# A fused HGRN2 attention and low-rank mixer: the hand-over from batch 0 to batch 1, with other steps between TensorE's products and with VectorE and ScalarE left to the scheduler

## The chip, the cores and the metric

One core of one Trainium2 chip runs the whole program. The metric is the device time of one execution in microseconds (us); lower is better. Five engines of the core matter here: TensorE (PE in the profile, its weight loads PEld), VectorE (DVE), ScalarE (ACT), GpSimd (POOL) and SyncE (SP), which issues nearly all the DMAs. Every engine executes its own instructions in order; the engines wait for each other with semaphores.

## The reference

Two blocks, one after the other, in float32. The attention block runs a gated recurrence over 768 steps for 4 batches of 8 heads of 48 columns; the mixer block mixes over time with a product of rank 32 and then over channels with two dense layers.

```python
batch, n_heads, seq, head_dim = (4, 8, 768, 48)
f = 1.0 / (1.0 + np.exp(-f_logit))
for t in range(S):
    state = f[:, :, t, :, None] * state + np.einsum('bhd,bhe->bhde', k[:, :, t], v[:, :, t])
    y[:, :, t] = np.einsum('bhd,bhde->bhe', q[:, :, t], state)
x = y.transpose(0, 2, 1, 3).reshape(B, S, H * D)          # (4, 768, 384)
u = x + (x.transpose(0, 2, 1) @ U @ V).transpose(0, 2, 1)  # U: 768 x 32, V: 32 x 768
ch = np.maximum(u @ w_ch1, 0.0) @ w_ch2                    # 384 -> 1536 -> 384
return u + ch
```

## The kernel before

**Units and batches.** Attention works in 16 units, each a pair of heads of one batch: unit n belongs to batch n // 4. A unit has a front and a rear. The front turns the inputs into operands: "gates" (the forget logits are transposed on VectorE, L766, and go through the sigmoid on ScalarE, L875 and L876), "keep" (a scan over time, L880, and four small operations, L885, L887, L888, L890), "keys" (a transpose L766 and a product L809), "read_back" (a second scan, L898) and "queries" (again L766 and L809). The rear computes scores, states and outputs on TensorE, with the scan of the states on VectorE (L1055) and copies on ScalarE (L1010, L1016, L1038, L1095).

**The mixer.** For each batch, `low_rank` forms x'U on TensorE (L184, tile ph) and ScalarE copies it out (L192, tile h); `added_up` adds its four parts with one product (L197) and ScalarE copies again (L199). `mix_blocks` multiplies by V (tile pu) and VectorE adds the result to x (L204): for batch 0 two blocks at a time, for the later batches four blocks at once in `mix_four` (L221) and then the last two (L214). `turn` transposes x on TensorE (L288, tile put), ScalarE copies the result to uT (L289). Then come the first dense layer, L300 (tile pz) with ReLU on ScalarE (L335), and the second one.

**Second products.** The 768 rows of a batch are six blocks of 128, taken as three pairs. A pair's second layer is either done plainly (L355, tile po) or, with sums of operands formed before, in seven instead of eight smaller products (L389, tile pw). Batch 0 does its first two pairs plainly and its third pair in seven. `seven` has four steps: step 0, 1 and 2 hold two products each (12 matmul instructions of the program, six per product), step 3 holds one. VectorE reads each step's pw with additions (L204, tiles w_y and o), and ScalarE copies one part of step 0 (L405). Step 1 needs a difference of second-layer weights that VectorE makes in place (L571), step 2 another (L572). Finished rows are stored by SP (L343).

**Around the change.** `start_mixer(1, after, early, late)` interleaves two things on TensorE: the end of batch 0 (`after`, the four steps of `seven` for its third pair) and the start of batch 1's mixer (`m.before`: `low_rank`, `added_up`, `mix_blocks`, three times `turn`). `early` and `late` are front pieces of the next units: read_back and queries of unit 9, gates and keep of unit 10. In the kernel before, `after` is `m.halved(...)`, seven pieces of one product each, so that `added_up` stands between the two products of step 1 and the mixing stands ahead of step 2.

**What sets the order.** TensorE's order is the order in which the program is written (`manual_schedule` for TensorE, over the whole kernel). VectorE's and ScalarE's order is the written order as well within an inner `manual_schedule` block, which in the kernel before reaches to the end of the first four pieces of batch 1's attention. After that block a scheduler orders VectorE and ScalarE by its own estimate of when operands are ready; additions marked `high_priority` (those through `add`) are favoured by it.

**Buffers.** The tiles pw, pu and put, and sc, y, ds and pt of attention, share three double-bank PSUM buffers (pool `ps_big`); ph, pz, po and two of the four tiles of `mix_four` share two single-bank ones (`ps_mm`). A buffer is written again when its last reader has finished. The tile `whole` (L1016) has one buffer, which the scan L1055 reads.

Of the kernel before, what the change touches and what calls it, by code (L numbers as in the profile page):

```python
# [576 lines left out]
def factored_path(ctx, tc, q, k, v, f_logit, moe_U, moe_V, moe_w_ch1, moe_w_ch2, out, ok):  # L577
# [10 lines left out]
    NBL = S // P  # L588
    HP = H // 2
# [29 lines left out]
    late = const.tile([P, 7, S], F32, name="late")  # L619
# [22 lines left out]
    def load(n, *names):  # L642

        b, hp = divmod(n, HP)
        for nm in names:
            if nm == "v":
                v_tiles[n] = three.tile([P, NBL, 2, D], F32, name="v_nat")
            for par in range(2):
                head = src[nm][b, 2 * hp + par]
                if nm in "kq" and n < HP:  # L650
                    if par == 0:
                        nc.sync.dma_start(
                            out=packed(n, nm).rearrange("p (h t) -> p h t", h=2),
                            in_=src[nm][b, 2 * hp : 2 * hp + 2].rearrange("h (p c) d -> p h (c d)", p=P),
                        )
                    continue
                if nm == "v" and par:

                    for s in range(2):
                        nc.sync.dma_start(  # L660
                            out=v_tiles[n][(1 - s) * C : (2 - s) * C, :, par, :],
                            in_=head.rearrange("(c s p) d -> s p c d", s=2, p=C)[s],
                        )
                    continue
                if nm == "v" or n < TURNED:
                    dst = v_tiles[n] if nm == "v" else nat[n % 2][nm]
                    nc.sync.dma_start(out=dst[:, :, par, 0:D], in_=head.rearrange("(c p) d -> p c d", p=P))
                    continue
                head = head.rearrange("(c i) d -> i c d", i=NB)
                for part in range(2):  # L670
                    p0 = par * PAD + part * NB
                    n_ch = min(NB, D - part * NB)
                    nc.sync.dma_start(
                        out=raw[n % 2][nm][p0 : p0 + NB, :].rearrange("p (c d) -> p c d", d=NB)[:, :, 0:n_ch],
                        in_=head[:, :, part * NB : part * NB + n_ch],
                    )
# [63 lines left out]
    early = len(weights)  # L740
# [169 lines left out]
    def mixer(b):  # L910
        return Mixer(tc, b, x_tiles[b], U, V, w1, w2, sums, ident, blocks, out, two, three, zp, ps_big, ps_mm,
                     b == 0, z_all, room if b >= B - 2 else None, FEWER - (b - B + 2) * NCH // 4)
# [11 lines left out]
    def sum_of_w(i):  # L924
        if i == 0:
            flat = late.rearrange("p a s -> p (a s)")
            w_places.extend(flat[:, j * FG : (j + 1) * FG] for j in range(7 * S // FG))
            w_places.extend(t[:, 0:FG] for t in fz + [added])
            flat = z_all[:, NFC:, :].rearrange("p i t -> p (i t)")
            w_places.extend(flat[:, j * FG : (j + 1) * FG] for j in range(3))  # L930
            assert max(W_PLACES) < len(w_places)
        n, p, sign, q = W_SUMS[i]
        nc.vector.tensor_tensor(w_node(n), w_node(p), w_node(q), ALU.add if sign == "+" else ALU.subtract)
# [171 lines left out]
    def front(n, *names):  # L1105

        if n >= NU:
            return []
        if n not in ahead:
            names_of = ("gates", "keep", "keys", "read_back", "queries", "gates_end", "unpack_k", "unpack_q")  # L1110
            ahead[n] = dict(zip(names_of, prepare(n)))
        return [ahead[n].pop(nm) for nm in names if nm in ahead[n]]

    def rear(n, *names):

        if not 0 <= n < NU:
            return []
        if n not in here:
            here[n] = dict(zip(("kept", "states", "scan", "scores", "read", "inner", "mask", "spread"), attend(n)))
        return [here[n].pop(nm) for nm in names if nm in here[n]]  # L1120

    def joined(*groups):

        groups = [g for g in groups if g]
        for _ in groups[1:]:
            yield lambda: None
        if groups:
            yield lambda: [f() for g in groups for f in g]

    def steps(first, last):  # L1130

        def behind(n):

            return HP + 3 <= n < NU - 1

        for n in range(first, last):
            if n < NU:
                yield from joined(rear(n - 2, "inner"), rear(n - 1, "scores"), rear(n, "kept"))
            else:
                for piece in rear(n - 2, "inner") + rear(n - 1, "scores"):  # L1140
                    yield lambda: None
                    yield piece
            if behind(n):
                yield from front(n, "read_back", "queries")
            if n + 1 < NU and n + 1 not in v_tiles:
                load(n + 1, "v")
            yield from front(n + 1, "gates", "keep", "keys")
            yield from joined(rear(n - 1, "read"), rear(n, "states", "scan"))
            if not behind(n + 1):
                yield from front(n + 1, "read_back", "queries")  # L1150
            if n + 1 == last:
                yield from rear(n - 1, "inner")
                if n + 2 < NU:
                    load(n + 2, "v")

    def attention(pieces, fill):

        for piece in pieces:
            fill()
            piece()  # L1160
        fill.rest()

    def beside(pieces, calls):

        for i, piece in enumerate(pieces):
            yield piece
            while calls and calls[0][0] <= i:
                calls.pop(0)[1]()
        assert not calls

    def start_mixer(b, after, early=(), late=()):

        m = mixer(b)
        n = len(after) // 4
        early, late = ([(0, f) for f in of] for of in (early, late))
        if late:
            pieces = after[:2] + m.before[:1] + early + after[2:3] + m.before[1:2] + after[3:4] + m.before[2:3] + late
            pieces += after[4:] + m.before[3:]
        else:
            pieces = after[:n] + m.before[:1] + after[n : 2 * n] + m.before[1:2] + after[2 * n : 3 * n]  # L1180
            pieces += m.before[2:3] + after[3 * n :] + m.before[3:]
        for _, piece in pieces:
            piece()
        return m
# [4 lines left out]
    with tc.manual_schedule(engines={nc.vector.engine, nc.scalar.engine}):  # L1189
# [21 lines left out]
        def room_for(first, last):  # L1211
            for i in range(first, last, 2):
                t = zp.tile([P, NFC // 2, 2 * P], F32, name="zw").rearrange("p i t -> p (i t)")
                nc.scalar.copy(t[:, 0:1], x_tiles[0][:, 0, 0:1])
                spare.extend([t.bitcast(U64)[:, 0:WP], t.bitcast(U64)[:, WP : 2 * WP]])
            for load_w in weights[early + first : early + last]:
                load_w[0]()
# [5 lines left out]
        for n in range(HP):  # L1223
            last = n + 1 == HP
            pieces = rear(n - 1, "scan") + front(n, "unpack_q", "keys") + rear(n, "spread") + rear(n - 1, "read")
            if last:
                pieces = [w[0] for w in weights[1:early]] + [lambda: room_for(0, 2)] + pieces + join[:1] + halves[1:2]
# [27 lines left out]
        m = mixer(0)  # L1255
# [44 lines left out]
            f()  # L1300
        first, third, others = to_sum
        todo = m.second(0) + [(0, first), (0, third)] + m.second(1)[:6] + m.ready(2) + m.second(1)[6:] + [(0, others)]
        after = m.halved(NBL // 2 - 1)

        attention(second, Fill(todo, 10 + 10 * HP - (len(start) + len(m.firsts) - 1 - EARLY)))
        n = 2 * HP + 2
        m = start_mixer(1, after, front(n - 1, "read_back", "queries"), front(n, "gates", "keep"))
        pieces, fill = steps(n - 1, 3 * HP + 1), Fill(m.main, 10 * HP - 3)
        for _ in range(4):
            fill()  # L1310
            next(pieces)()
    for b in range(2, B - 1):
        if b > 2:
            pieces, fill = steps(b * HP + 1, (b + 1) * HP + 1), Fill(m.main, 10 * HP)
        after = m.after
        attention(pieces, fill)
        m = start_mixer(b, after)
# [3 lines left out]
    for i in range(early_sums):  # L1321
        sum_of_w(i)
    pieces = beside(steps((B - 1) * HP + 1, NU + 1),
                    [(t, lambda i=i: sum_of_w(i)) for i, t in enumerate(turns, early_sums)])
# [375 lines left out]
```

## Time and profile before

| | |
|---|---|
| median of 3 runs | 473.17 us (472.33 to 473.63) |
| the profiled execution | 473.17 us, of which 471.4 us are the span from its first to its last instruction |
| busy, PE / DVE / ACT / POOL | 96% / 76% / 35% / 11% of the span |
| granted TensorE clock | 1.0 |
| DMA | 34.37 MB, 73 GB/s over the span |

The span can be cut at the place of the change. Batch 0's last products and the start of batch 1's mixer lie between 150 and 172 us. The costliest groups of the page show what the kernel's time consists of; each line gives the program line, the engine, the operation, the tiles, the number of instructions, the busy time and the mean of one in ns, and after the bar the idle time before them and what ended it:

```profile
L300 PE MATMUL pz<-uT,w 128*128 128x256 f32 x492 | 111.6, 382 | 0.3 <-DVE w_y L204 0.2
L389 PE MATMUL pw<-w,z_all 128*128 128x192 f32 x228 | 39.5, 327 | 0.0
L389 PE MATMUL pw<-zw,w_raw 128*128 128x192 f32 x168 | 30.1, 329 | 1.9 <-DVE zw L571 1.9
L880 DVE TENSOR_TENSOR_SCAN late<-fz,late 128x768 f32<-128x768 f32 x12 | 21.1, 1754 | 12.0 <-ACT fz L875 11.9
L898 DVE TENSOR_TENSOR_SCAN late<-fz,other 128x768 f32<-128x768 f32 x12 | 22.0, 1835 | 0.1
```

A matmul of the program on float32 operands shows as two records of the trace. Matmul durations overlap, so the pace of a run of them is read from their starts, not from the mean of one.

### The profile page before, as it was taken

The page shows a single profiled execution, that of the slowest core. Times are in us where ns is not written, and L with a number is a line of the kernel's source. Part 1 is how long each engine was busy: PE and PEld are TensorE (multiplying, and loading weights), DVE is VectorE, ACT ScalarE, POOL GpSimd, SP SyncE. Part 2 cuts the span into 40 slices and gives each one's busy share as a digit, 9 for nine tenths or more (in the row PEclk, how much of TensorE's full clock was granted, in tenths as well). Part 3 has the DMA queues.
Part 4 walks back from the last instruction along what each step waited for, and adds up shares of the span by engine and source line. Part 5 has one row for each costly group of instructions (what it writes and reads, how often), then busy time and mean ns, then how long its engine had stood idle before and what let it go on. Part 6 is the DMA issues. An engine that isn't in the chain of part 4 may idle for free.

```text
span 471.4 us, 13114 instructions
## 1 busy us (share of the span) xinstructions
PE 454.6 (96%) x5675; PEld 400.2 (85%) x5675; DVE 357.9 (76%) x596; ACT 166.3 (35%) x320; POOL 53.9 (11%) x60
## 2 busy tenths in 40 slices
PE   8998999999979789999999999999999999999996
PEld 6886888876657678899898888989989999999996
DVE  5768788979999957766756568977897896858652
ACT  6775776562332034322322323431221311112200
POOL 2002445634110100101010100120000000000000
PEclk9999999999999999999999999999999999999999
DMA  9939998587667533503542130100000000000001
GB/s 198 203 109 214 217 216 177 147 124 102 111 96 110 84 60 42 84 6 75 74 64 60 26 60 3 27 4 19 19 2 1 33 1 19 18 0 35 1 34 39
DMA packets 148584, 34.37 MB, mean 73 GB/s; under 512 B 136934, under 2 KB 146982, under 8 KB 148518
## 3 DMA queue, kind: packets, MB, share of 16 engines
q1 hardware_dynamic: 147718, 33.29, 36.5%
q8 instruction: 47, 0.77, 0.7%
q10 hardware_dynamic: 800, 0.15, 0.2%
q14 instruction: 19, 0.16, 0.1%
HBM read 28.70 MB, written 4.72 MB: 71 GB/s over the span
## 4 chain that ended last, share of the span: by engine, by line
PE 77%; DVE 15%; issue 4%; ACT 2%; DMA 1%; POOL 0%; SPq 0%; DVEq 0%; ACTq 0%; POOLq 0%
PE pw L389 24%; PE pz L300 20%; PE pp L496 12%; PE po L355 5%; PE y L1071 2%; PE sc L979 2%; PE ds L1030 2%; PE y L1089 2%; PE pt L789 2%; PE pt L839 1%; DVE w_raw L204 1%; PE pt L1006 1%; DVE added L1055 1%; DVE late L880 1%; DVE x L204 1%
## 5 line engine op out<-in xcount | busy, mean ns | idle before, releaser
L300 PE MATMUL pz<-uT,w 128*128 128x256 f32 x492 | 111.6, 382 | 0.3 <-DVE w_y L204 0.2
L300 PEld LDWEIGHTS pz<-uT,w 128*128 128x128 f32 x492 | 91.7, 190 | 13.1 <-PE pw L389 0.5
L1059 POOL COPY st<-added 128x576 f32<-128x576 f32 x12 | 17.8, 1484 | 193.4 <-DVE added L1055 193.4
L389 PE MATMUL pw<-w,z_all 128*128 128x192 f32 x228 | 39.5, 327 | 0.0
L389 PEld LDWEIGHTS pw<-w,z_all 128*128 128x128 f32 x228 | 37.2, 190 | 0.6
L101 POOL TENSOR_TENSOR w<-w_y,w_r 128x384 int32<-128x384 int32 x24 | 31.5, 1311 | 37.0 <-DVE w_y L100 22.5
L335 ACT ACTIVATE z_all<-pz 128x512 f32<-128x512 f32 x33 | 19.6, 596 | 40.6 <-PE pz L300 40.2
L389 PE MATMUL pw<-zw,w_raw 128*128 128x192 f32 x168 | 30.1, 329 | 1.9 <-DVE zw L571 1.9
L880 DVE TENSOR_TENSOR_SCAN late<-fz,late 128x768 f32<-128x768 f32 x12 | 21.1, 1754 | 12.0 <-ACT fz L875 11.9
L389 PEld LDWEIGHTS pw<-zw,w_raw 128*128 128x128 f32 x168 | 27.3, 190 | 2.7 <-issue 2.2
L489 ACT ACTIVATE other<-other 128x512 f32<-128x512 f32 x18 | 11.3, 631 | 40.3 <-DVE other L204 40.3
L992 DVE TENSOR_TENSOR A<-sc,causal 128x768 f32<-128x768 f32 x16 | 15.2, 951 | 13.5 <-PE sc L979 13.5
L898 DVE TENSOR_TENSOR_SCAN late<-fz,other 128x768 f32<-128x768 f32 x12 | 22.0, 1835 | 0.1
L875 ACT ACTIVATE fz<-late 128x756 f32<-128x756 f32 x10 | 8.3, 832 | 33.8 <-DVE late L766 33.8
L489 ACT ACTIVATE z_all<-z_all 128x512 f32<-128x512 f32 x12 | 7.6, 631 | 34.1 <-DVE z_all L204 34.1
L1038 ACT COPY added<-ds 48x576 f32<-48x576 f32 (+2 forms) x29 | 17.8, 618 | 4.7 <-PE ds L1030 4.2
L496 PE MATMUL pp<-v_nat,late 128*128 128x128 f32 x152 | 19.1, 275 | 0.0
L98 DVE TENSOR_SCALAR w_y<-w_y 128x384 f32<-128x384 f32 (+3 forms) x27 | 12.1, 448 | 8.9 <-ACT w_y L91 8.9
L1071 PEld LDWEIGHTS y<-st,qT 48*64 48x64 f32 x704 | 13.6, 137 | 6.0 <-issue 3.9
L389 PE MATMUL pw<-w,other 128*128 128x192 f32 x108 | 18.5, 326 | 0.0
L1016 ACT COPY whole<-whole 128x576 f32<-128x576 f32 x16 | 10.8, 672 | 21.3 <-DVE added L1055 21.1
L496 PEld LDWEIGHTS pp<-v_nat,late 128*128 128x128 f32 x152 | 18.0, 192 | 0.0
(234 smaller groups left out, 913.0 us busy)
## 6 DMA issues: line engine op xcount, KB each, us to landing
w_raw<-in_moe_w_ch_dram SPq DMA_DIRECT2D x18, 384.0 KB, 3.7
out_dram<-o SPq DMA_DIRECT2D x17, 192.0 KB, 1.9
v_nat<-in_v_dram SPq DMA_DIRECT2D x16, 144.0 KB, 3.0
v_nat<-in_v_dram SPq DMA_DIRECT2D x32, 72.0 KB, 3.5
zw<-in_moe_w_ch_dram SPq DMA_DIRECT2D x6, 384.0 KB, 4.8
out_dram<-o SPq DMA_DIRECT2D x14, 96.0 KB, 2.2
w<-in_k_dram SPq DMA_DIRECT2D x4, 288.0 KB, 3.7
w<-in_q_dram SPq DMA_DIRECT2D x4, 288.0 KB, 4.7
```

The source lines that it names most:

```text
L101: nc.gpsimd.tensor_tensor(dst.bitcast(I32), shaped(y.bitcast(I32)), shaped(r), ALU.add)
L300: nc.tensor.matmul(pm[:, i * 2 * P : (i + 1) * 2 * P], lhsT=w1[:, m, o : o + P], rhs=uT[a][:, m, :], start=(m == 0), stop=(m == NDC - 1))
L335: nc.scalar.activation(z[a, c][:, k : k + 2, :].rearrange("p i t -> p (i t)"), pm, AF.Relu)
L355: nc.tensor.matmul(pm, lhsT=z[a, i // NI][:, i % NI, s * P : (s + 1) * P], rhs=w2[:, i, :], start=(i == 0), stop=(i == NFC - 1))
L389: nc.tensor.matmul(W["pm"][:, n * HM : (n + 1) * HM], lhsT=lhs[:, i, :], rhs=rhs[i] if isinstance(rhs, list) else rhs[:, i, :], start=(i = ...
L489: nc.scalar.activation(dst, dst, AF.Relu, scale=float(SIGNS[n]))
L496: nc.tensor.matmul(pm[:, i, r * P : (r + 1) * P], lhsT=room["w"](wn)[:, r * P : (r + 1) * P], rhs=x_node(a, xn), start=((xn, wn) == of[0]) ...
L880: nc.vector.tensor_tensor_scan(backwards(X, S - 1, S), backwards(f, S, S), backwards(ends, S - 1, S), 0.0, ALU.mult, ALU.add,)
L898: nc.vector.tensor_tensor_scan(Y, f[:, 0:S], starts, 0.0, ALU.mult, ALU.add)
L1038: nc.scalar.copy(added[r, 1:].rearrange("p (e c s) -> p e c s", c=NBL, s=2)[:, e], ds[r, :, 0 : NBL * D].rearrange("p s (c e) -> p e c s", ...
L1059: nc.gpsimd.tensor_copy(st, states.rearrange(by_e, c=NCH))
L1071: nc.tensor.matmul(o(c % 2, par, c // 2), lhsT=T["q"][rows[par], chunk[c]], rhs=T["st"][rows[par], c, :], start=(c <= 2), stop=False, skip ...
```

## The change

`halved` is no longer used here: `after` is `m.after`, the four whole steps of `seven`. `start_mixer` has one order for all batches; `early` follows `low_rank`, `late` follows step 2 and stands ahead of the mixing. The call of `start_mixer(1, ...)` and the first four pieces of batch 1's attention leave the inner block, so that the scheduler orders VectorE and ScalarE there. The mixing of batch 1 is done four blocks at once before and after.

```diff
         m = mixer(b)
         n = len(after) // 4
         early, late = ([(0, f) for f in of] for of in (early, late))
-        if late:
-            pieces = after[:2] + m.before[:1] + early + after[2:3] + m.before[1:2] + after[3:4] + m.before[2:3] + late
-            pieces += after[4:] + m.before[3:]
-        else:
-            pieces = after[:n] + m.before[:1] + after[n : 2 * n] + m.before[1:2] + after[2 * n : 3 * n]
-            pieces += m.before[2:3] + after[3 * n :] + m.before[3:]
+        pieces = after[:n] + m.before[:1] + early + after[n : 2 * n] + m.before[1:2] + after[2 * n : 3 * n] + late
+        pieces += m.before[2:3] + after[3 * n :] + m.before[3:]
         for _, piece in pieces:
             piece()
         return m
...
-        after = m.halved(NBL // 2 - 1)
+        after = m.after
 
         attention(second, Fill(todo, 10 + 10 * HP - (len(start) + len(m.firsts) - 1 - EARLY)))
-        n = 2 * HP + 2
-        m = start_mixer(1, after, front(n - 1, "read_back", "queries"), front(n, "gates", "keep"))
-        pieces, fill = steps(n - 1, 3 * HP + 1), Fill(m.main, 10 * HP - 3)
-        for _ in range(4):
-            fill()
-            next(pieces)()
+    n = 2 * HP + 2
+    m = start_mixer(1, after, front(n - 1, "read_back", "queries"), front(n, "gates", "keep"))
+    pieces, fill = steps(n - 1, 3 * HP + 1), Fill(m.main, 10 * HP - 3)
+    for _ in range(4):
+        fill()
+        next(pieces)()
```

Built, the two programs hold the same compute instructions, and their order differs in this stretch alone:

| engine | order before | order after |
|---|---|---|
| TensorE | step 0, L184, half of step 1, L197, other half, mixing L221 and L214, step 2, step 3, L288 | step 0, L184, step 1, L197, step 2, mixing L221 and L214, step 3, L288 |
| VectorE | keys of unit 9 (L766, L809), po's o, L1055, L571, L572, step 0, L898, L766 and L809 of unit 9's queries, step 1, four additions to x, L766, L880 and the small ones of unit 10, step 2, L898 of unit 10, step 3 | L766 of unit 9's keys, L898, L809, po's o, L766 and L809 of unit 9's queries, L1055, L571, L572, L766 of unit 10, step 0, L880 and the small ones, L898 of unit 10, step 1, step 2, four additions to x, step 3 |
| ScalarE | L405, L192, L199, L875, L876, three L289, two L335, L1010, L1016 | L1016, L405, L875, L192, L876, L199, three L289, two L335, L1010 |
| SyncE | four issues of L673 for f of unit 12, four stores L343 | two stores, the four issues of L673, two stores |
| GpSimd | | the same |

In the buffers, step 2 takes the double bank of the tile ds instead of that of step 1; the four mixed blocks take step 0's, the last two blocks step 1's, step 3 takes step 2's; and the three put tiles take those of the four mixed blocks, of the last two, and of step 3 (before: of the last two blocks, of step 2, and of the first put itself).

## The prediction

> **What bounds the kernel now.** I read the page first, then the window table around the change, then the chain that ended last, in order of time, through it.
>
> ```profile
> PE 454.6 (96%) x5675; PEld 400.2 (85%) x5675; DVE 357.9 (76%) x596; ACT 166.3 (35%) x320; POOL 53.9 (11%) x60
> PE 77%; DVE 15%; issue 4%; ACT 2%; DMA 1%; POOL 0%; SPq 0%; DVEq 0%; ACTq 0%; POOLq 0%
> ...
> 150.50:172.00 21.50, 17.06 (x141) 14.35 (x139) 20.32 (x30) 3.33 (x7) 2.18 (x1) 1.00 0.50 74
> 172.00:245.00 73.00, 73.00 (x972) 65.85 (x971) 47.51 (x63) 25.13 (x45) 3.62 (x3) 1.00 0.38 59
> ```
>
> TensorE bounds the whole, but not the stretch of the change. The window lines give the stretch, its length, and then the busy time of PE, PEld, DVE, ACT and POOL: from 150.5 to 172 PE is idle for 4.4 of 21.5 us and DVE is busy for 20.3; from 172 to 245 PE is not idle at all. So batch 1's first L300 is the gate: what it starts later, the 73 us behind it end later. The chain through the stretch (start, length, what):
>
> ```profile
> 152.94 1.27 DVE added L1055
> 154.21 1.26 DVE zw L571
> ...
> 158.30 1.75 DVE late L898
> ...
> 163.43 2.66 DVE x L204 x4
> 166.08 0.90 DVE late L766
> ...
> 170.66 0.27 DVE w_y L204
> ...
> 171.07 0.96 PE put L288 x24
> 172.03 5.38 PE pz L300 x24
> ```
>
> Nearly all of it is DVE; PE enters at 171.07, behind step 2's last addition. PE's timeline (start, length, what, and in brackets the idle time and who ended it) and the list of its waits show where it stood:
>
> ```profile
> 152.54 1.18 PE L184 MATMUL ph<-x,U 128*32 128x384 f32 x16
> 155.61 2.19 PE L389 MATMUL pw<-zw,w_raw 128*128 128x192 f32 x12 [1.89 <-DVE zw L571]
> 162.62 2.22 PE L389 MATMUL pw<-w,zw 128*128 128x192 f32 x12 [0.74 <-DVE o L204]
> 171.07 0.96 PE L288 MATMUL put<-ident,x 64*128 64x64 f32 x24 [1.81 <-DVE w_y L204]
> ...
> PE pt L1006 <- DVE kz L809: 2.6, 1, 2.6
> ```
>
> The three bracketed waits are the 4.4 us; 2.6 is the longest wait of PE anywhere. Behind 172 its waits sum to 1.1 us (0.4, 0.3, 0.2, 0.2), and the chain holds no DMA, so nothing is left there to swallow a delay: one us at L300 is one us at the end.
>
> **The change part by part.** No instruction is added or removed, so the price is all order. I walk VectorE in its new order from 150.51, the start of unit 9's L766, with the distance from one start to the next as the timeline of before has it.
>
> *VectorE up to L571.* L766 0.89, L898 1.67, L809 0.88, po's o 0.46, queries L766 0.98 and L809 0.88, L1055 1.27: L571 starts at 157.54 instead of 154.13. The 3.4 us are L898 and the queries (1.67 + 0.98 + 0.88), which stood behind step 0 before. There is no idle time on DVE to hide them. L571 takes 1.33, and PE started 0.15 after its end: step 1 starts at 159.0 instead of 155.61. L184, which ends at 153.7, is all that PE has until then, so its wait grows from 1.9 to 5.3 us.
>
> *VectorE from L571 on.* 1.37 to L572, 2.16 to L766 of unit 10 (161.07), whose output is there at 162.04; in between the two additions of step 0 (to 162.68) fill what was idle time. ScalarE's L875 takes 0.83, so L880 starts at 162.95, after 0.27 us idle (0.90 before). L880 to L898 is 2.32 (182.00 to the end of L888 at 184.30 in unit 11), L898 1.67: step 1's additions start at 166.94. They and step 2's take 0.38, 0.37, 0.27, 0.54, 0.46 and end at 169.3; the four additions to x start at 169.23 and end at 171.95 (2.66 and 0.07). The last two put tiles follow 0.14 later, and L300 0.89 after that: 173.0 against 171.96. In short: L898 of unit 10 (1.67) now stands ahead of L300 instead of behind it, and 0.63 of idle time is saved; 1.04 in sum. VectorE has the same work in both, but PE now waits for all of it.
>
> *TensorE.* Step 1 from 159.0 takes 4.09 (as step 0, 148.45 to 152.54): 163.1. L197 waits for h: on ScalarE the copy L192 is now queued behind L875, which waits for L766 of unit 10; 162.07 + 0.74 + 0.48 = 163.3. L197 0.65, step 2 4.0, mixing 1.4: 169.4, just when step 2's buffer is free for step 3 (169.3). Step 3 2.05, first put 0.59, copy to uT 0.80, two hops of 0.05: 172.9. So TensorE alone gives +0.95, and the two paths end within 0.1 us: what slows either counts in full. Two waits vanish (0.74 for step 1's buffer, 1.81 ahead of put), one of 0.2 for h is new, and the one of 1.89 grows by 3.4: the balance, +1.05, agrees.
>
> *ScalarE, SyncE, GpSimd.* L1016 now stands ahead of L405 and waits for L1055 to give `whole` free (157.6). Behind it wait L405 (done 158.6, needed by VectorE at 161.96), then L875 and L192 as above: cost 0.2 us on PE, already counted. Without VectorE's queue as cover it would be 5 us on h (153.79 before). SyncE's load of f for unit 12 moves behind two stores, from 167.0 to about 170.8; it is read at 198.25, so it costs nothing. POOL's copy L1059 still starts with L571.
>
> *The rate behind the long wait.* A wait of 5.3 us is not in the trace of before. The nearest rows: behind its longest wait (2.6) PE ran at full pace, the twelve L355 records took 4.14 us or 0.35 each; at the opening, where it came from standing still, six records of the same 384 columns took 4.21 or 0.70 each, and L839 fell from 0.42 to 0.28 of length only at 6.4 us:
>
> ```profile
> 1.07 4.21 PE L1196 MATMUL idle<-late 128*128 128x384 f32 x6 [1.07 <-DVE late L679]
> 5.31 2.36 PE L839 MATMUL pt<-later,late 128*128 128x130 f32 x12
> 138.44 4.14 PE L355 MATMUL po<-w,z_all 128*128 128x384 f32 x12
> ```
>
> The granted clock reads 1.00 in both places, so the lengths are the witness. The opening lost half of 5.4 us, 2.7. Bounds: 0 to 2.7. I take 1.3, half of it: the wait is twice the longest harmless one, but it interrupts an engine at full pace instead of starting one. Sum: 172.9 + 1.3 = 174.2, +2.2 us: span 473.6, and with the 1.8 us around it (473.17 - 471.4) 475.4. The profiled execution is the median run, so this is the forecast for the median too.
>
> [...]
>
> **The rivals.**
>
> *Order only (A).* The rate survives the wait, and the 1.04 us stand alone: 474.2, own range 473.6 to 474.9. For: the clock row never falls below 1.00. Against: the opening's lengths.
>
> *The other side: PE's two later waits were the price (B).* If L571 were done as early as before, the step 1 wait stayed at 1.9, and the 0.74 and 1.81 would be gone: 473.17 - 2.55 = 470.6, faster. It decides from the point where VectorE's three moved operations find 2.4 us of slack ahead of 154. For: those waits do vanish by the new order. Against: DVE is busy for 4.90 of the 5 us from 150 to 155.
>
> *A further stall (C).* Step 1's start at 159.0 leaves step 3 and the put tiles bound to the last additions; if hops between DVE, PE and ACT there cost one more round of step 3 (2.05) beyond the lost rate: 477.5. Against: each hop above has a measured length.
>
> *Nothing arrives (D).* The words of the change name four blocks mixed at once, which batch 1 does already; and if the reordering only moved the waits within the same 4.4 us, it stays 473.2. Against: L898 ahead of L300.
>
> **How the numbers follow.** Forecast 0.45 (own range 474.4 to 476.7), A 0.38, B 0.08, C 0.05, D 0.04. 0.3% is 1.42 us, about what measurements of this kernel can tell from no change; the border to slower is 474.59. Slower: 0.43 of the forecast's 0.45, 0.11 of A, all of C: 0.59. Same: 0.02 of the forecast, 0.27 of A, D: 0.33. Faster: B, 0.08. The range 473.1 to 476.9 takes in D and leaves out B, C and some 0.06 at the edges.
>
> **What would show it.** Right: in the changed profile PE waits some 5.3 us for zw L571 after L184, the waits for o and w_y are gone, and the first L300 of batch 1 starts at 173 or later. If the rate fell, step 1's first L389 records are longer than 326 ns and their starts lie twice as far apart, while the clock may read 1.00. If they are 326 ns throughout, A holds. L571 starting by 155 would show B; a wait at step 3 or put of over 1 us, C; L300 at 172, D. Idle time of PE behind 173 that differs from the 1.1 us of before would break the claim that a delay passes to the end unchanged.

## The result, and the profile after

Beside each other on one chip the changed kernel took 476.22 us (475.7 to 476.89, 4 runs) and the kernel before 473.09 us (472.33 to 473.63, 4 runs): a ratio of 1.0068, 95% interval 1.0049 to 1.0087, or 3.1 us more. The span grew from 471.4 to 474.3 us.

From the page of the changed kernel, the first lines, and of the rows in 40 slices those of PE and of the granted clock:

```profile
span 474.3 us, 13116 instructions
PE 457.0 (96%) x5675; PEld 402.9 (85%) x5675; DVE 358.0 (75%) x596; ACT 166.4 (35%) x320; POOL 54.0 (11%) x60
PE   8999999999979599999999999999999999999997
PEclk9999999999999799999999999999999999999999
```

What matters is slice 14 of 40 (154 to 166 us): PE falls to 5 tenths there, and in the row of the granted clock a 7 stands where the kernel before had a 9. PE's busy time is 2.4 us longer for the same 5675 instructions: some of them ran slowly.

The waits of PE in the stretch and behind it (who waited for whom, us, times, longest):

```profile
PE pw L389 <- DVE zw L571: 5.3, 1, 5.3
PE ds L1030 <- ACT seen L1078: 0.4, 1, 0.4
PE y L1071 <- POOL st L1059: 0.3, 1, 0.3
PE pz L300 <- DVE w_y L204: 0.2, 1, 0.2
```

The waits for o (0.7) and w_y (1.8) ahead of L300 are gone, the one for L571 is 5.3 instead of 1.9, and from L300 on the waits are those of before. PE's timeline through the stretch (start, length, what, idle time before it):

```profile
152.91 1.18 PE L184 MATMUL ph<-x,U 128*32 128x384 f32 x16
159.35 4.18 PE L389 MATMUL pw<-zw,w_raw 128*128 128x192 f32 x12 [5.26 <-DVE zw L571]
163.32 2.56 PE L389 MATMUL pw<-w_r,w_raw 128*128 128x192 f32 x12
...
175.48 5.45 PE L300 MATMUL pz<-uT,w 128*128 128x256 f32 x24
```

Twelve records of step 1 take 4.18 us where twelve of before took 2.19. The window table of the changed kernel (stretch, its length, busy time of PE, PEld, DVE, ACT, POOL, then the granted clock) tells why:

```profile
154.00:157.00 3.00, 0.09 (x4) 0.00 (x0) 2.97 (x5) 0.00 (x0) 0.00 (x0) 1.00 0.76 113
157.00:159.00 2.00, 0.00 (x0) 0.00 (x0) 2.00 (x2) 0.89 (x2) 0.92 (x1) 0.60 0.70 140
159.00:162.00 3.00, 2.65 (x8) 2.68 (x9) 2.96 (x3) 0.00 (x0) 1.25 (x1) 0.50 0.90 122
162.00:164.00 2.00, 2.00 (x8) 2.00 (x8) 1.69 (x4) 1.32 (x3) 0.00 (x0) 0.50 0.00 0
164.00:165.00 1.00, 1.00 (x7) 1.00 (x6) 1.00 (x1) 0.00 (x0) 0.00 (x0) 0.89 0.00 0
```

The clock falls to 0.50 at about 157.4, 3.3 us into the wait, and is back at about 164.2: 6.8 us, of which PE works 4.9 at a clock of 0.50 and so loses 2.4. All four executions of the changed kernel have the same mean clock over the span, 0.993. L300 starts at 175.48 instead of 171.96. The profile reaches the stretch 0.37 us later already (unit 9's L766 starts at 150.87 instead of 150.51), so the stretch itself costs 3.15 us, which is the whole loss. In both profiles the last matmul of the kernel ends 295.42 us behind this L300. (That the span grew by 2.9 us and not by 0.37 + 3.15 lies behind the last matmul, where the profile of before took 4.05 us and that of after 3.44.)

### The profile page after: what moved, and what is told of

Same layout as the page of the kernel before. It is cut to its first block, busy times and chain, and to the rows that moved or that the text cites. A ratio compares the mean times of both kernels' runs of the same rounds, so it can differ in the third digit from the quotient of the medians.

```text
span 474.3 us, 13116 instructions
## 1 busy us (share of the span) xinstructions
PE 457.0 (96%) x5675; PEld 402.9 (85%) x5675; DVE 358.0 (75%) x596; ACT 166.4 (35%) x320; POOL 54.0 (11%) x60
## 4 chain that ended last, share of the span: by engine, by line
PE 79%; DVE 11%; issue 4%; ACT 2%; DMA 1%; SPq 1%; POOL 0%; DVEq 0%; ACTq 0%; POOLq 0%
PE pw L389 26%; PE pz L300 20%; PE pp L496 12%; PE po L355 5%; PE y L1071 2%; PE y L1089 2%; PE sc L979 2%; PE ds L1030 2%; PE pt L789 2%; PE pt L839 1%; DVE w_raw L204 1%; PE pt L1006 1%; DVE added L1055 1%; DVE late L933 1%; PE idle L1192 1%
## 5 line engine op out<-in xcount | busy, mean ns | idle before, releaser
L300 PE MATMUL pz<-uT,w 128*128 128x256 f32 x492 | 111.6, 382 | 0.5 <-DVE w_y L204 0.2
L300 PEld LDWEIGHTS pz<-uT,w 128*128 128x128 f32 x492 | 91.7, 190 | 13.3 <-ACT uT L289 0.6
L1059 POOL COPY st<-added 128x576 f32<-128x576 f32 x12 | 17.8, 1484 | 196.6 <-DVE added L1055 196.6
L389 PE MATMUL pw<-w,z_all 128*128 128x192 f32 x228 | 39.5, 327 | 0.0
L389 PEld LDWEIGHTS pw<-w,z_all 128*128 128x128 f32 x228 | 37.2, 190 | 0.6
L389 PE MATMUL pw<-zw,w_raw 128*128 128x192 f32 x168 | 32.1, 343 | 5.3 <-DVE zw L571 5.3
L389 PEld LDWEIGHTS pw<-zw,w_raw 128*128 128x128 f32 x168 | 29.1, 200 | 6.1 <-issue 5.6
L335 ACT ACTIVATE z_all<-pz 128x512 f32<-128x512 f32 x33 | 19.6, 596 | 39.8 <-PE pz L300 39.3
L880 DVE TENSOR_TENSOR_SCAN late<-fz,late 128x768 f32<-128x768 f32 x12 | 21.0, 1754 | 11.4 <-ACT fz L875 11.3
L898 DVE TENSOR_TENSOR_SCAN late<-fz,other 128x768 f32<-128x768 f32 x12 | 22.0, 1833 | 0.2
L1016 ACT COPY whole<-whole 128x576 f32<-128x576 f32 x16 | 10.8, 674 | 29.0 <-DVE added L1055 28.8
L875 ACT ACTIVATE fz<-late 128x756 f32<-128x756 f32 x10 | 8.3, 832 | 29.9 <-DVE late L766 29.9
L389 PE MATMUL pw<-w,other 128*128 128x192 f32 x108 | 18.5, 326 | 0.0
```

The lines of the kernel that those rows point to most:

```text
L300: nc.tensor.matmul(pm[:, i * 2 * P : (i + 1) * 2 * P], lhsT=w1[:, m, o : o + P], rhs=uT[a][:, m, :], start=(m == 0), stop=(m == NDC - 1))
L335: nc.scalar.activation(z[a, c][:, k : k + 2, :].rearrange("p i t -> p (i t)"), pm, AF.Relu)
L389: nc.tensor.matmul(W["pm"][:, n * HM : (n + 1) * HM], lhsT=lhs[:, i, :], rhs=rhs[i] if isinstance(rhs, list) else rhs[:, i, :], start=(i = ...
L880: nc.vector.tensor_tensor_scan(backwards(X, S - 1, S), backwards(f, S, S), backwards(ends, S - 1, S), 0.0, ALU.mult, ALU.add,)
L898: nc.vector.tensor_tensor_scan(Y, f[:, 0:S], starts, 0.0, ALU.mult, ALU.add)
L1059: nc.gpsimd.tensor_copy(st, states.rearrange(by_e, c=NCH))
```

## The experiments

The kernels ran in three sets, those of a set on the same chip and with the kernel before beside them. In these sets the kernel before spread more than at first (set 1: 471.94 to 475.3, median 474.08; set 2: 472.42 to 476.07, 473.69; set 3: 471.25 to 478.7, 473.47), so small differences need their interval.

### Set 1: the two halves of the change, and work in the wait

**Seven products in the wait.** The added lines, in `products`, ahead of step 1 of batch 0's third pair; the fourth kernel of this set has a 3 for the 7:

```diff
+            if b == 0 and a == NA - 1 and of[0][0] is S.get((a, 2)) and 0 in parts:
+                for _ in range(7):
+                    nc.tensor.matmul(W["pm"][:, 0:DM], lhsT=ident, rhs=w1[:, 0, 0:DM], start=True, stop=True)
             for n in parts:
                 lhs, rhs = of[n]
```

With these lines the scheduler also moves two VectorE operations by one or two places (one addition of step 2 and the L766 of the next unit).

> The changed kernel, with seven products of 128 x 384 (ident by columns of w1, into the PSUM tile that step 1 overwrites) between L184 and step 1, so that TensorE's wait of 5.26 us is work for some 4.8 us (0.69 each). They change no output. Theory (the long wait costs the clock, and the order of the rest costs 1.0 us): the granted clock stays at 1.00, step 1's L389 records are 326 ns from the first, the first L300 of batch 1 starts at about 173.3 in place of 175.5, and the time is 474.0 to 474.4, about 2.1 us under the changed kernel. Rival (VectorE's order alone costs all of the 3.1 us, the slow clock lies beside other work): 476.2, L300 at 175.5 with a clock of 1.00.

Measured: 474.34 us, ratio to the kernel before 1.0017 (0.9999 to 1.0034), +0.8 us instead of +3.1. The clock stayed at 1.00 through the wait, and the first twelve records of step 1 took 2.11 us where the changed kernel's took 4.18. So most of the loss is not VectorE's order as such. The profile is not as clean as hoped: the clock was at 0.50 elsewhere, from 139.0 to 142.4, behind the 2.57 us wait of L1006 that all these kernels have. PE came late to the stretch by 1.9 us and the seven products then overran VectorE by about 1 us.

**TensorE's order alone.** The changed kernel, with its call of `start_mixer(1, ...)` and the pieces behind it put back into the inner block:

```diff
-    n = 2 * HP + 2
-    m = start_mixer(1, after, front(n - 1, "read_back", "queries"), front(n, "gates", "keep"))
...
+        n = 2 * HP + 2
+        m = start_mixer(1, after, front(n - 1, "read_back", "queries"), front(n, "gates", "keep"))
```

> TensorE's new order alone: batch 1's start stays in the block in which VectorE and ScalarE keep the written order. L571 is then as early as in the kernel before, so TensorE waits some 1.9 us for it and the clock stays at 1.00. Theory: unit 10's scan L880 stands ahead of the four additions to x, which end at about 172.0 as in the changed kernel; L300 at 173.0 and a time of 474.1. Rival (TensorE's order brings the loss): 476. Second rival (VectorE's order brings all of it): 473.1, as the kernel before.

Measured: 476.05 us, ratio 1.0034 (1.0018 to 1.005), +1.6 us. The wait for L571 is short as expected (0.24 us) and two waits for the additions to x ahead of put take its place (2.26 and 1.21 us). Its profile, that of the longest of its twelve executions (479.86 us), has falls of the clock at 41.0 to 51.3 us, at 143.4 to 146.8 and, behind those two waits, at 177.6 to 181.0, so it doesn't separate order from clock: the second rival (all of it VectorE's order) falls, the first one is left open at half strength. The mean clocks of the executions say a little more. Six read 0.992 or 0.993 and have a median of 474.74 us; 14 of the 29 of the kernel before beside it read 0.991 to 0.994, with a median of 474.43. The other six read 0.982 or 0.986, with 477.2. So where the clock is alike, TensorE's order makes no difference beyond the scatter, and half of the executions pay for a slower clock.

**The scheduler's order alone.** The kernel before with only the call moved out of the inner block; TensorE keeps its old order, with step 1 and the mixing split.

```diff
         after = m.halved(NBL // 2 - 1)
...
-        n = 2 * HP + 2
-        m = start_mixer(1, after, front(n - 1, "read_back", "queries"), front(n, "gates", "keep"))
...
+    n = 2 * HP + 2
+    m = start_mixer(1, after, front(n - 1, "read_back", "queries"), front(n, "gates", "keep"))
```

> The scheduler's order of VectorE and ScalarE alone: TensorE keeps the order of the kernel before, step 1 and the mixing split as there. L571 starts some 3.4 us late, TensorE waits 5.3 us in front of step 1 and the granted clock falls to 0.50 as in the changed kernel. Theory: 475.7 to 476.7, the same loss as with the whole change, clock 0.993 over the span. Rival (both parts are needed): 474 to 474.5.

Measured: 476.44 us, ratio 1.0057 (1.0038 to 1.0076), +2.7 us. PE waits 5.26 us for L571, to the digit as in the changed kernel, and the clock is at 0.50 from 157.5 to 164.3. Moving the call out of the block is enough for the long wait, the fall and nearly all of the loss.

**Three products in the wait.**

> As with seven, but three of the 128 x 384 products in front of step 1: TensorE works until some 2.1 us into the wait and then stands for about 3.2 us. This asks how long a wait the clock bears. [...] If 2.6 us, the longest wait of the kernel before, is near the limit, it falls and the time is 475.5 to 476.5; if it falls in some runs only, the runs lie in two groups.

Measured: 474.45 us, ratio 1.0007 (0.9993 to 1.0021). Because of the fall at 138 PE came late here too, and the rest of the wait was 1.48 us and not 3.2; the clock stayed at 1.00 in it. So how long a wait the clock bears was not answered by this run; the last section has the waits ahead of the falls in all profiles.

### Set 2: the clock and the order apart

To be rid of the fall at 138, three kernels of this set carry three such products in that wait, too (`kept` of unit 8, overwritten by its transposes):

```diff
             pt = ps_big.tile([P, 2, 512], F32, name="pt", tag="big")
+            if n == 2 * HP:
+                for _ in range(3):
+                    nc.tensor.matmul(pt[:, 0, 0:DM], lhsT=ident, rhs=w1[:, 0, 0:DM], start=True, stop=True)
             for c in range(NBL):
```

The changed kernel as it is:

> The changed kernel itself, beside the next three on one chip. In the profiles of the runs so far a second fall of the granted clock shows, at 138 to 143 us, behind the wait of 2.6 us of L1006 that the kernel before has too; in the first profiles of both kernels it is not there. Theory: 476 to 477 on this chip, a fall to 0.50 for some 6.8 us in the wait for L571 in every profile, the one at 138 in some.

The kernel before with the early products:

> The kernel before with three 128 x 384 products (ident by columns of w1, overwritten by the transposes behind them) in its 2.6 us wait at 135 to 138 us. They change no output. Theory (the fall at 138 comes from that wait, in some of the executions): no fall in the profile, 472.3 to 473.0, and less spread than the kernel before beside it, which gains about 1 us. Rival (that fall has another cause or costs nothing): same as the kernel before within 0.3 us.

The changed kernel with early products and five in the wait for L571:

> The changed kernel with three such products at 135 us and five in the wait for L571. Theory: clock 1.00 throughout, and what is left against f2_before_early is the price of the order alone, 1.0 us: 473.3 to 474.0. Rival (order alone costs nothing, all of the loss is the clock): equal to f2_before_early within 0.4 us. Second rival (order costs 3 us): 475.3 or more.

The changed kernel with the early products only:

> The changed kernel with three such products at 135 us only. The difference to f3_after_both is the price of the slow clock in the wait for L571. Theory: 2.1 to 2.4 us above f3_after_both, 475.5 to 476.2, clock 0.993. Rival (the slow clock is mostly covered by VectorE): under 1 us above f3_after_both.

Measured, with the first L300 counted from the start of step 0 in the same profile:

| kernel | median us | ratio to before (95%) | step 0 to L300 | clock in the wait |
|---|---|---|---|---|
| before (the step from the profile of the first comparison) | 473.69 | | 23.51 | 1.00 |
| before, early products | 473.35 | 1.0003 (0.9988 to 1.0019) | 24.13 | 1.00 |
| changed, both | 474.14 | 1.0007 (0.9991 to 1.0024) | 24.80 | 1.00 |
| changed, early products | 476.02 | 1.0044 (1.0023 to 1.0065) | 26.85 | 0.50 for 6.8 us |
| changed | 475.34 | 1.0037 (1.0012 to 1.0062) | 24.26 | 0.50 for 3.4 us |

The rows two to four are the comparison: the fourth becomes the third by filling the wait for L571, and the third differs from the second by the change with that wait filled. Filling the wait: 476.02 to 474.14, 1.9 us, or 2.05 by L300; that is the price of the clock. What is left of the change with the clock held: 474.14 to 473.35, 0.8 us, or 1.29 by L300 against the first profile of before; that is the price of the order. The intervals of single ratios are 0.7 to 1.2 us to either side, so these are sizes, not third digits. Of the expectations, the time of the fourth row is in its range; the third row lies 0.14 us above its own; the fifth is a miss, 0.7 us below its range and with a shorter fall.

The mean granted clock that is on record for every execution makes the comparison cleaner. One stretch of 3.4 us at 0.50 takes 0.0036 off it (half of 3.4 us in a span of 474 us), and the counts of stretches here and below are estimates from that. All ten executions of the fourth row read 0.993, which is two such stretches (6.8 us in its profile). Of the twelve of the third row eleven read 0.999 or 1.00, none; of the twelve of the second row four read 1.00 and eight 0.995 or 0.996, one. The plain kernel before read under 0.998 in 95 of its 97 executions of the three sets. So its medians contain slow stretches, and a ratio to it flatters a kernel that has none. Between the executions without such a stretch the order costs 474.14 - 473.02 = 1.1 us. One correction belongs here: in the profiles of the kernels with products in the wait for L571 a wait of 0.2 us of a later L300 (at 252 us in the kernel before) is gone, and the last matmul ends 295.0 us behind batch 1's first L300 instead of 295.4. So 0.4 us of what filling the wait gains in the medians is not the clock, and the order is dearer by as much. Taken together the order costs 1.1 to 1.5 us and the clock 1.5 to 2.05.

The window table of the changed kernel with both fillings, and that of the one with the early filling:

```profile
153.00:160.00 7.00, 5.16 (x29) 3.15 (x22) 6.93 (x8) 0.89 (x2) 2.18 (x1) 1.00 0.73 120
160.00:164.00 4.00, 3.77 (x22) 3.21 (x21) 3.69 (x5) 1.32 (x3) 0.00 (x0) 1.00 0.35 42
```

```profile
158.00:159.00 1.00, 0.00 (x0) 0.00 (x0) 1.00 (x2) 0.09 (x1) 0.00 (x0) 0.76 0.67 137
159.00:165.00 6.00, 4.73 (x15) 4.76 (x16) 5.66 (x6) 2.13 (x5) 2.16 (x1) 0.50 0.54 77
165.00:166.00 1.00, 1.00 (x7) 1.00 (x6) 0.96 (x2) 0.00 (x0) 0.00 (x0) 0.83 0.00 0
```

VectorE is about as busy in both; what differs is the clock, and the five products that hold it up. The chain of the kernel with both fillings, ahead of L300:

```profile
160.95 0.98 DVE late L769
161.92 0.02 issue
161.94 0.84 ACT fz L878
162.78 0.37 ACT h L192
163.16 0.04 issue
163.20 0.91 PE ph L197 x2
164.11 3.90 PE pw L392 x24
168.01 0.86 PE pu L221 x8
168.87 0.63 PE pu L214 x4
169.50 2.15 PE pw L392 x12
171.65 0.54 PE put L288 x12
172.19 0.02 issue
172.21 0.81 ACT uT L289
173.02 0.04 issue
173.06 5.45 PE pz L300 x24
```

(Behind the added lines the numbers are shifted by three: L392 is L389, L769 is L766, L878 is L875.) This is TensorE's path of the prediction, piece by piece: L766 of unit 10, the sigmoid, the copy of h behind it, L197 and the rest without a gap, and L300 at 173.06, where the prediction's two paths ended at 172.9 and 173.0. (Just ahead of these lines the view names a DMA that landed at 160.92. VectorE's queue explains the start of L769 without it: it lies 2.17 us behind that of L575, as L766 lies 2.15 us behind L572 in the changed kernel.)

The early products did not show a gain: the kernel before with them is 0.3 us under the kernel before by the medians, within the interval, and its spread is no smaller (472.43 to 475.94). Its own profile has a fall at another place, from 172.5 to 176, behind the 1.82 us wait for w_y; that made the first L300 group 6.49 us long instead of 5.45.

### Set 3: the two weight differences on GpSimd

If VectorE's queue is what bounds the hand-over, L571 and L572 could leave it, since GpSimd is idle there (for 13.96 us, up to L1059 at 154.34):

```diff
-        sub(sums[2], q[1, 1], sums[1], ALU.subtract)
-        sub(sums[4], q[1, 0], sums[2], ALU.subtract)
+        nc.gpsimd.tensor_tensor(sums[2], q[1, 1], sums[1], ALU.subtract)
+        nc.gpsimd.tensor_tensor(sums[4], q[1, 0], sums[2], ALU.subtract)
```

The kernel before with the first of the two lines, and with both:

> The kernel before with L571 on GpSimd, which stands idle from 140.4 to 154.3 us, in place of VectorE. By L101 (1.31 us for 128 x 384) it takes about 3.9 us there, from about 146.5, when the last plain product has freed its tile. Theory (VectorE's queue bounds the hand-over): the chain through VectorE is 1.37 us shorter, TensorE's wait for L571 is gone, L300 starts at about 170.6, 471.5 to 472.2 against 473.1 to 474.1 before. Rival (GpSimd slows VectorE beside it, or GpSimd's copy L1059 comes too late): no gain.

> The kernel before with both L571 and L572 on GpSimd: about 7.8 us there, from 146.5 to about 154.5, and the copy L1059 right behind. Theory: VectorE's chain is 3.5 us shorter, L300 starts at about 168.5, and no wait of TensorE in the stretch is over 1.9 us; 469.5 to 471, faster than both kernels. Rival (GpSimd becomes the bound of step 2, or slows VectorE): 472 or more.

Measured: 474.02 us, ratio 0.9992 (0.9962 to 1.0022), and 475.66 us, ratio 1.0036 (1.0013 to 1.0058). A miss, and the rival has it: beside the two operations on GpSimd two operations of VectorE took much longer. VectorE's timeline of the second kernel, then GpSimd's:

```profile
148.55 4.19 DVE L880 TENSOR_TENSOR_SCAN late<-fz,late 128x768 f32<-128x768 f32 x1
152.77 2.42 DVE L885 COPY least<-late 128x12 f32<-128x12 f32 x1
155.11 0.16 DVE L887 TENSOR_SCALAR X<-late 128x12 f32<-128x12 f32 x1
```

```profile
148.39 2.73 POOL L571 TENSOR_TENSOR zw<-w,zw 128x1152 f32<-128x1152 f32 x1 [7.71 <-PE po L355]
151.20 3.96 POOL L572 TENSOR_TENSOR w<-w,zw 128x1152 f32<-128x1152 f32 x1
```

L880 takes 4.19 instead of 1.75 us and ends 1.62 us behind L571 (which ends at 151.12); L885, a copy of 12 columns, takes 2.42 instead of 0.17 and ends at 155.19, 0.03 us behind L572. L572 itself, of the same shape as L571, takes 3.96 us where L571 took 2.73, and ends 2.42 us behind L880. What holds the operations up is not shown. VectorE loses 4.7 us to be spared 3.6 (1.33 and 2.24). With L571 alone on GpSimd it is L885 that takes 2.42 us, so VectorE loses 2.25 us to be spared 1.33. In the second kernel the clock adds to the loss: step 2 waits 2.34 us for o, the clock is at 0.50 from 165.5 to 168.9, and the two products of step 2 take 5.7 us instead of 4.0.

The changed kernel with both on GpSimd, and with L571 alone:

> The changed kernel with L571 and L572 on GpSimd; the scheduler's order of VectorE and ScalarE is the same otherwise. Theory (the loss comes from the scheduler putting three operations of unit 9 ahead of L571 in VectorE's queue): TensorE no longer waits for L571, the clock stays at 1.00 in the stretch, the longest wait is some 2 us, for h (L192 behind L875 on ScalarE); L300 at about 169.5, 470 to 471.5. Rival (the loss lies in the order of the rest): it stays 1 us or more above g2_before_sums_pool with the clock at 1.00, that is 471 to 474.

> The changed kernel with L571 alone on GpSimd: step 1 then waits for nothing of VectorE, step 2 waits for L572 (VectorE, about 159.8 by its new start) behind step 1 and L197. Theory: no wait over 3 us, clock 1.00 in the stretch, VectorE's chain 1.37 us shorter than with the order alone: L300 at about 171.7, 472 to 473. Rival (clock falls all the same): 474 to 475.5.

Measured: 477.4 us, ratio 1.0077 (1.0054 to 1.0101), and 476.08 us, ratio 1.0057 (1.0036 to 1.0077). A miss as well, by the same GpSimd operations and by one more step: the wait for L571 is gone in both, as expected, but the one for h has grown in its place. PE's timeline of the first of the two:

```profile
156.09 2.11 PE L389 MATMUL pw<-w_r,w_raw 128*128 128x192 f32 x12
163.15 1.65 PE L197 MATMUL ph<-h,blocks 128*128 128x384 f32 x2 [4.95 <-ACT h L192]
164.59 4.05 PE L389 MATMUL pw<-w,zw 128*128 128x192 f32 x12
```

ScalarE has L1016 ahead of L405, L875 and L192, and L1016 starts only behind L1055, at 161.03. The wait of 4.95 us costs the clock again: 0.50 from 162.0 to 168.8, step 2's first half 4.05 us instead of 2.1. With L571 alone the wait is 2.71 us and the clock falls for 3.4 us all the same. So the fall came behind waits for ScalarE (4.95 and 2.71 us) as it came behind the one for VectorE (5.26 us).

No kernel here beats the kernel before beyond its interval.

## Why the prediction was right

The forecast was 475.4 us (own range 474.4 to 476.7, range 473.1 to 476.9); measured 476.22. Its mechanism held; the size of one term did not.

- *VectorE up to L571.* Forecast 157.54, measured 157.87, which is 157.50 without the late start of 0.37. (The three moved operations sum to 3.53 us and not to the 3.4 of the text; the walk itself has the 3.41.) The wait was forecast at 5.3 and is 5.26 us. The scheduler's order alone gave the same wait.
- *VectorE from L571 on.* L880 was forecast at 162.95 behind 0.27 us idle; it started at 163.25 (162.88) behind 0.27. With the clock held, L300 came at 173.06 against 173.0.
- *TensorE's path and the order's price.* +0.95 to +1.04 was forecast; 1.29 us by L300, 0.8 by medians and 1.1 between executions without a fall were measured with the clock held, so it is near the forecast or a little above it. Rival A as a time (474.2) is what that kernel shows (474.14), but on a chip where the kernel before took 473.69.
- *The rate behind the wait.* This is the mis-sized term of the sum: 1.3 was taken, half of what the opening lost (2.7). In the changed profile PE lost 2.4 us, and filling the wait was worth 2.05 by L300 and 1.5 to 1.9 by medians: above the middle of 0 to 2.7, by L300 well above it. The reason given for the half, that the wait interrupts an engine at full pace instead of starting one, did not hold: the clock stayed low 4.9 us into the work, nearly as long as the 5.4 of the opening. By L300 it accounts for 0.75 of the 0.8 us between forecast and measurement; by medians for less, and the order for the rest.
- *How often the rate falls.* Whether it would fall at all the prediction left open (the forecast 0.45, order only 0.38). The clock reads 0.993, by the estimate above two slow stretches, in all four executions of the changed kernel and in all ten of the one with the early products; in the profiles of both it is at 0.50 for 6.8 us.
- *The clock row.* The prediction said that the row might read 1.00 during a fall, as it does in the opening. It read 0.50. Only the opening is not marked: the clock record of these two profiles begins at 6.9 and 7.2 us.
- *ScalarE.* "Without VectorE's queue as cover it would be 5 us on h": where L571 no longer covered it, the wait for h was 4.95 us.
- *The delay passes to the end.* Behind L300 the waits of 0.4, 0.3 and 0.2 us are the same, and so is the distance to the end of the last matmul (295.42 us); 3.15 us in the stretch, 3.1 us in the median.
- *The rivals.* B fell: VectorE had no slack ahead of 154. C and D fell: no wait behind step 1 but those forecast, and L300 did move.

Not settled: what TensorE's order alone costs. Its run is 1.6 us over the kernel before (0.8 to 2.4); where the clock is alike it is 0.3 us over it, within the scatter, and its one profile does not show which falls of the clock the order brings in the other executions.

## What to carry to other kernels

Here a wait of TensorE cost its own length and then a clock of 0.50 for 3.4 us or more, in every profile with a wait of 3.57 us or longer and in some with one of 1.8 to 2.7 us; in a stretch where TensorE alone is on the path, price both, and price the second at half the time that TensorE works at the low clock (2.4 us for 4.9 in the changed kernel). Compare executions with the same mean clock before putting a small difference down to the order. Before freeing an engine from a written order, follow the longest-awaited operation through its new queue: a scheduler that fills a queue with ready work can put that work ahead of the one operation that another engine waits for. Before moving work to an idle GpSimd, look at what a VectorE operation beside it takes (here 2.42 instead of 0.17 us for a copy of 12 columns).

## What was not expected of the hardware

**The clock also fell behind waits of 1.8 to 2.7 us.** All falls seen go to 0.50 and last 3.4, 6.8 or, once, 10.2 us. They came behind waits of 5.26, 5.35, 4.95 and 3.57 us in every profile that had one, but also behind 2.71 us, behind 2.34 us, behind 2.57 us at 138 us (in eight profiles of the later sets, in neither of the first two) and once behind 1.82 us. In the changed kernel's second profile the fall starts over 1 us after PE has resumed:

```profile
138.00:139.00 1.00, 0.62 (x13) 0.59 (x13) 1.00 (x2) 0.00 (x0) 0.00 (x0) 1.00 0.95 128
139.00:143.00 4.00, 4.00 (x8) 2.13 (x9) 4.00 (x5) 1.37 (x2) 1.21 (x1) 0.57 0.98 127
143.00:160.00 17.00, 13.43 (x201) 9.89 (x200) 16.80 (x21) 3.91 (x8) 1.82 (x1) 1.00 0.72 114
160.00:164.00 4.00, 4.00 (x17) 4.00 (x16) 3.69 (x5) 1.32 (x3) 0.35 (x1) 0.57 0.47 55
```

PE resumes at 138.38, and the clock is at 0.50 from about 139.5 to 143.0. In the five profiles with more than one fall, falls start whole multiples of 3.413 us apart, to within 0.02 us as the window tables give the times. The two above, at 139.54 and 160.02, are six times 3.413 apart. The others are thirty (TensorE's order alone, 41.02 and 143.42), eight (the kernel before with both differences on GpSimd, 138.18 and 165.50), seven (the changed kernel with both, 138.06 and 161.96) and eight (with L571 alone, 137.38 and 164.68). What sets these times is not shown.

Within the kernels there are 18 falls. In 17 of them the 3.41 us up to the fall held 1.75 us or more without PE work; the least were 1.75 us (the fall at 137.38) and 1.82 us (the kernel before with the early products, 172.75). In the kernel before the 3.41 us from 153.70 held 1.89 us of it, and no fall came. The same wait of 2.57 us at 138 had a fall behind it in one profile and none in another. In the kernel before, two stretches of 3.41 us, counted back from the change of its clock at 471.14, hold 1.54 and 1.28 us without PE work, and no clock falls (first two lines); in the changed kernel's second profile the 3.41 us up to the fall hold 2.25 us of it, and the next 3.41 are slow (last two lines):

```profile
133.22:136.64 3.42, 1.88 (x97) 1.49 (x96) 3.03 (x6) 2.25 (x6) 0.00 (x0) 1.00 0.85 137
136.64:140.05 3.41, 2.13 (x17) 1.54 (x18) 3.38 (x5) 1.37 (x2) 0.88 (x1) 1.00 0.74 96
136.13:139.54 3.41, 1.16 (x14) 0.97 (x15) 3.38 (x6) 0.48 (x1) 0.00 (x0) 1.00 0.64 98
139.54:142.95 3.41, 3.41 (x7) 1.70 (x6) 3.41 (x4) 0.89 (x2) 1.21 (x1) 0.50 1.02 131
```

The lengths differ with PE's idle time, too. Twelve falls lasted 3.4 us, and PE was idle for less than 0.1 us in them; five lasted 6.8 us, and PE was idle for 1.1 us or more in their first 3.4 us. One fall fits neither: that at 41.0 us in the kernel with TensorE's order alone came behind 3.41 us with 1.0 us of idle time and lasted 10.2 us; it stays open.

The wider spread of the later sets goes with it. In set 2 the ten executions of the kernel before whose mean clock tells of one slow stretch have a median of 473.24 us, the twenty with two 473.95, the three with three 474.80. In the first comparison only the profiled execution of the kernel before has its clock on record, 1.00; why it had no fall and nearly all of the later ones had is not known.

**In that profile the early fall softens the later one.** It makes PE late for the stretch, so that the wait for L571 is 3.57 instead of 5.26 us and the second fall half as long (3.4 us); the kernel with the early wait filled, and thus without the first fall, was not faster (476.02 against 475.34).

**Operations of VectorE took longer beside subtractions on GpSimd.** A 12-column copy took 2.42 instead of 0.17 us beside one, a scan 4.19 instead of 1.75. GpSimd's took longer as well: L572 3.96 us and, alone on GpSimd, L571 4.20, where L571 took 2.73 in the kernel before with both. Why is not shown.
